# Reordered first loads, four PSUM banks for the first tile, a shorter attention lead and gated later loads in a linear-attention + MLP kernel

## The chip, the cores and the metric

One NeuronCore of one Trainium2 chip runs the whole program. The metric is device time in microseconds (us), the median over all runs of a kernel. A ratio is the mean time of one kernel's fast runs over the mean of the other's in the same rounds, so it is not quite the ratio of the medians that are quoted.

## The reference, cut to what matters

```python
batch, heads, seq, head_dim = 8, 8, 576, 64        # attention, 128 random features
q_s, k_s = q * 64**-0.25, k * 64**-0.25
def phi(x):                                        # x @ omega.T, minus |x|^2/2, minus the row max, exp
    h = einsum('bhsd,md->bhsm', x, omega) - sum(x*x, -1)/2
    return exp(h - max(h, -1)) / sqrt(128)
kv  = einsum('bhsm,bhsd->bhmd', phi(k_s), v)
num = einsum('bhsm,bhmd->bhsd', phi(q_s), kv)
den = einsum('bhsm,bhm->bhs',  phi(q_s), sum(phi(k_s), 2)) + 1e-6
x   = (num / den) as 4608 tokens x 512
h   = x @ w_in                                     # 512 -> 2048
out = (h * sigmoid(beta * h)) @ w_out              # 2048 -> 512, float32
```

## The kernel before: the parts that matter

The program is a list of operations with dependencies. A small list scheduler in the kernel's own source orders them for each engine by estimated durations; on the chip each engine then runs its list strictly in that order and waits on semaphores. There are 8 batches of attention. Batch b gives the transposed x (`xT`) of MoE tile b; a ninth tile collects the leftover tokens. A tile has 16 "up" groups (4 matmuls each, then tanh on ACT and a multiply on DVE) and 16 "down" groups (4 matmuls each).

```python
NAT_BUFS, T_BUFS, E_BUFS, Q_BUFS, V_BUFS, KV_BUFS, X_BUFS = 2, 2, 2, 2, 2, 2, 2
PE_T, PE_XT = 2, 3     # batches under 2: k and q transposed on PE; under 3: x too; later ones by DMA on SP
WARM = 24              # idle matmuls, meant to keep the PE clock up in the prologue
LEAD = 62              # attention may run that many MoE groups ahead
P0, O0, C0, H0 = 0, 2, 4, 6      # PSUM banks: projections, down, kv/num, up
# [...]
load("v", 0)           # v of batch 0: raw float32, issued by SP
load("k", 0)           # everything else: casting loads, issued by POOL, in this order
load("q", 0)
for c in range(4):
    load_w_in(c)
load("k", 1)
load("q", 1)
load_w_out(0)
load("v", 1)
for c in range(1, 4):
    load_w_out(c)
# [...] in attention(b): a gate is a number of MoE groups that the scheduler must have placed already
gates = [max(0, 32 * b - 16 - LEAD + 16 * half) if b >= 2 else 0 for half in range(2)]
# [...] b >= PE_T: one DMA transpose each for k and q
dma("SP", 4.0, 3.2, lambda e, x=x: e.dma_start(tr[x][:, st, :, :], nat[x][:, sn, :], transpose=True),
    reads=keys, writes=[...], gate=gates[0], lag=T_LAG)
# [...] up(t, f)
hb, ts, gs = H0 + u % 2, u % TH_BUFS, t % G_BUFS
# [...] down(t, sub, g4)
ob, os_, gs = O0 + u % 2, u % O_BUFS, t % G_BUFS
```

A gate is not a wait on the chip. It only says how late the scheduler puts an operation into its engine's list. For a load this is POOL's list, in which loads stand between the operations that scale v (`vsc`).

The softmax here doesn't subtract the row's maximum and nothing guards it: scores larger than these inputs give would overflow.

## Time and profile before

339.72 us (339.22 to 340.04); the profiled execution has a span of 337.9 us.

| stage | what limits it |
|---|---|
| 0 to 33.8 us, the prologue | the chain of batch 0: k's load, exponentials, x transposes |
| 33.8 to 333.9 us | PE, hardly waiting |
| the last 4 us | last eviction and store |

These are the waits of PE in the kernel before, from 33.8 us to the end (who waited for whom: us in total, times, longest):

```profile
PE ps L632 <- ACT xT L361: 0.8, 1, 0.8
PE ps L655 <- DVE g_sb L645: 0.6, 1, 0.6
```

L632 is the up matmul and L655 the down matmul. In 300 us PE waits 1.4 us. The windows view of the same kernel says it again; the columns are the stretch, its length, busy us of each engine (with its instructions), the granted PE clock, the DMA share as the view gives it (it can exceed 1) and GB/s:

```profile
60.00:80.00 20.00, 19.88 (x142) 10.30 (x141) 8.46 (x15) 11.81 (x20) 4.62 (x7) 1.00 1.37 179
80.00:120.00 40.00, 39.40 (x330) 23.42 (x329) 30.03 (x58) 31.83 (x59) 20.65 (x31) 1.00 1.44 166
160.00:180.00 20.00, 20.00 (x150) 10.46 (x148) 14.18 (x27) 11.14 (x18) 5.35 (x8) 1.00 0.75 125
180.00:220.00 40.00, 40.00 (x289) 22.28 (x288) 24.97 (x50) 29.45 (x54) 8.53 (x12) 1.00 0.37 85
```

The prologue, by the timeline (start, duration, engine, line, operation, and in brackets the idle time before it with its releaser):

```profile
9.72 0.82 PE L382 MATMUL ps<-identb,k_nat 128*128 128x128 bf16 x6 [5.64 <-DMA k_nat<-in_k_dram]
13.27 1.46 PE L382 MATMUL ps<-identb,k_nat 128*128 128x128 bf16 x12 [1.04 <-DMA k_nat<-in_k_dram]
...
23.76 2.21 ACT L441 ACTIVATE qpT<-ps 128x1024 bf16<-128x1024 f32 x3 [0.49 <-PE ps L426]
...
33.78 1.90 PE L632 MATMUL ps<-xT,w_in_bf 128*128 128x512 bf16 x8 [0.80 <-ACT xT L361]
```

PE waits 5.6 us for k, the q exponentials end at 26.0 us, and the first up matmul starts at 33.78 us. And two lines of its DMA issues (queue, count, KB each, median us from issue to landing):

```profile
k_nat<-in_k_dram POOLq DMA_DIRECT2D x4, 80.0 KB, 6.6
...
kT<-k_nat SPq DMA_TRANSPOSE x6, 12.1
```

The first line is k of batch 0. The second, the DMA transpose of k, takes 12.1 us to land in the median.

### The profile page before, as it was taken

To read this page: it belongs to the slowest core of one execution; us is meant where nothing else is said; L and a number is where in the kernel's file an instruction comes from. 1 tells how busy PE (TensorE), PEld (TensorE's weight loads), DVE (VectorE), ACT (ScalarE), POOL (GpSimd) and SP (SyncE) were. 2 spreads that over 40 slices of the span, in tenths; PEclk is the share of its full clock that TensorE was granted. 3 is DMA by queue.
4 is the path that set the end of the run, shared out by engine and by line. 5 is a ranking of instruction groups with operands and counts; after the bars stand their busy time and mean duration, and the time that the engine had idled before them with its cause. 6 is when DMAs were issued, how large, how long until landed. Compare 5 with 4: busy or idle time off the path is not lost.

```text
span 337.9 us, 5498 instructions
## 1 busy us (share of the span) xinstructions
PE 319.5 (95%) x2214; PEld 170.6 (50%) x2214; DVE 190.7 (56%) x358; ACT 204.0 (60%) x349; POOL 107.2 (32%) x161
## 2 busy tenths in 40 slices
PE   0597999999999999999999999999999999999995
PEld 0364565554655555665554565465444444444442
DVE  0196598428767769877854675765643333444400
ACT  2274668468886888788746876766444445444511
POOL 8859648215386262833500312303000000000000
PEclk9999999999999999999999999999999999999999
DMA  7999999999999999897196173221210001100033
GB/s 140 203 205 197 203 197 176 165 168 166 187 117 150 228 198 172 117 177 92 24 204 154 36 139 70 72 67 36 71 63 33 31 31 41 55 31 31 33 79 76
DMA packets 81113, 39.16 MB, mean 116 GB/s; under 512 B 47792, under 2 KB 76480, under 8 KB 81088
## 3 DMA queue, kind: packets, MB, share of 16 engines
q0 software_dynamic: 33280, 17.77, 41.2%
q1 hardware_dynamic: 47808, 21.05, 33.7%
q8 instruction: 17, 0.28, 0.4%
q14 instruction: 8, 0.07, 0.1%
HBM read 36.77 MB, written 9.44 MB: 137 GB/s over the span
## 4 chain that ended last, share of the span: by engine, by line
PE 87%; DVE 4%; ACT 3%; DMA 2%; POOL 1%; issue 0%; DVEq 0%; POOLq 0%
PE ps L655 36%; PE ps L632 35%; PE ps L418 4%; PE ps L426 4%; PE ps L546 3%; PE ps L521 2%; DMA k_nat<-in_k_dram 2%; POOL k_nat L254 1%; PE ps L382 1%; ACT E_sb L437 1%; ACT th_sb L641 1%; DVE g_sb L645 1%; DVE mk L474 1%; PE ps L580 1%; PE ps L595 1%; PE ps L516 1%
## 5 line engine op out<-in xcount | busy, mean ns | idle before, releaser
L645 DVE SCALAR_TENSOR_TENSOR g_sb<-th_sb,ps 128x512 bf16<-128x512 f32 x144 | 98.4, 685 | 92.5 <-ACT th_sb L641 91.9
L632 PE MATMUL ps<-xT,w_in_bf 128*128 128x512 bf16 x576 | 147.1, 379 | 0.8 <-ACT xT L361 0.8
L655 PE MATMUL ps<-w_out_bf,g_sb 128*128 128x512 bf16 x576 | 144.0, 379 | 0.7 <-DVE g_sb L645 0.6
L641 ACT ACTIVATE th_sb<-ps,beta_sb 128x512 f32<-128x512 f32 x144 | 99.1, 688 | 74.5 <-PE ps L632 73.8
L655 PEld LDWEIGHTS ps<-w_out_bf,g_sb 128*128 128x128 bf16 x576 | 55.5, 98 | 58.9 <-DVE g_sb L645 1.1
L632 PEld LDWEIGHTS ps<-xT,w_in_bf 128*128 128x128 bf16 x576 | 54.9, 98 | 53.8 <-DVE g_sb L645 1.0
L493 POOL TENSOR_TENSOR vsc<-v_nat,mk 128x512 bf16<-128x512 bf16 x28 | 28.8, 1050 | 88.2 <-DVE mkm L471 79.2
L437 ACT ACTIVATE E_sb<-ps 128x512 bf16<-128x512 f32 (+2 forms) x76 | 41.2, 573 | 18.4 <-PE ps L418 17.9
L441 ACT ACTIVATE qpT<-ps 128x512 bf16<-128x512 f32 (+2 forms) x76 | 41.4, 572 | 8.3 <-PE ps L426 7.4
L665 ACT ACTIVATE o_sb<-ps 128x512 f32<-128x512 f32 x36 | 21.5, 598 | 21.1 <-PE ps L655 21.0
L418 PE MATMUL ps<-bd,kT 128*128 128x256 bf16 x144 | 27.5, 291 | 1.6 <-ACT E_sb L437 0.9
L254 POOL DMA_DIRECT2D k_nat<-in_k_dram x36 | 22.5, 665 | 14.5 <-DMA kT<-k_nat 13.1
L561 DVE TENSOR_TENSOR xn<-ps,rden 128x640 bf16<-128x640 f32 x32 | 26.2, 820 | 0.7
L426 PE MATMUL ps<-qT,bd 128*128 128x256 bf16 (+2 forms) x152 | 25.7, 267 | 0.0
L418 PEld LDWEIGHTS ps<-bd,kT 128*128 128x128 bf16 x144 | 13.5, 103 | 12.4 <-ACT E_sb L437 2.4
L426 PEld LDWEIGHTS ps<-qT,bd 128*128 128x128 bf16 x152 | 13.7, 98 | 11.3 <-ACT qpT L441 0.8
L254 POOL DMA_DIRECT2D v_nat<-in_v_dram x28 | 17.6, 667 | 0.9 <-POOL vsc L506 0.8
L546 PEld LDWEIGHTS ps<-kvs,qpT 128*128 128x128 bf16 x320 | 13.7, 97 | 6.7 <-DVE kvs L537 0.9
L474 DVE TENSOR_TENSOR mk<-own,mkm 128x4 f32<-128x4 f32 x16 | 16.2, 1015 | 0.3
L452 DVE TENSOR_TENSOR mt<-E_sb 128x1152 bf16<-128x1152 bf16 x16 | 13.0, 811 | 4.3 <-ACT E_sb L437 4.1
L546 PE MATMUL ps<-kvs,qpT 128*128 128x65 bf16 x320 | 14.8, 193 | 0.3 <-DVE kvs L537 0.3
L269 POOL DMA_DIRECT2D q_nat<-in_q_dram x8 | 7.8, 975 | 15.7 <-DMA qT<-q_nat 14.4
(48 smaller groups left out, 155.0 us busy)
## 6 DMA issues: line engine op xcount, KB each, us to landing
out_dram<-o_sb SPq DMA_DIRECT2D x32, 256.0 KB, 2.4
q_nat<-in_q_dram POOLq DMA_DIRECT2D x8, 512.0 KB, 12.6
k_nat<-in_k_dram POOLq DMA_DIRECT2D x14, 160.0 KB, 12.5
v_nat<-in_v_dram POOLq DMA_DIRECT2D x14, 160.0 KB, 11.3
w_in_bf<-in_moe_w_in_dram POOLq DMA_DIRECT2D x4, 512.0 KB, 12.9
w_out_bf<-in_moe_w_out_dram POOLq DMA_DIRECT2D x4, 512.0 KB, 14.5
k_nat<-in_k_dram POOLq DMA_DIRECT2D x14, 128.0 KB, 12.5
v_nat<-in_v_dram POOLq DMA_DIRECT2D x14, 128.0 KB, 11.2
```

The lines of the kernel that those rows point to most:

```text
L254: lambda e: e.dma_start(dst[lo : lo + 64, g : g + group, c0 * D : (c0 + n) * D], srcap),
L418: i = e.matmul(view[:, c * 256 : c * 256 + 256], tr["k"][:, st, c0 + c, :], bd[:, :, :].rearrange("p a m -> p (a m)"), start=True, stop=Tr ...
L426: i = e.matmul(view[:, a * w : a * w + nch * 128], bd[:, a, :], tr["q"][:, st, c0 : c0 + nch, :], start=True, stop=True, skip_group_check= ...
L437: ex = lambda e: e.activation(dst[:, slot, s0 : s0 + 2 * nch, :].rearrange("p c m -> p (c m)"), view[:, 0 : nch * 256], AF.Exp)
L441: ex = lambda e: e.activation(dst[:, slot, s0 : s0 + 2 * nch, :].rearrange("p (c a) m -> p a c m", a=2), view.rearrange("p (a c) -> p a c" ...
L493: lambda e, pr=pr: e.tensor_tensor(vsc[:, sv, pr, 0:8, 0:D].rearrange("p (h j) d -> p h j d", h=2), ends(vs[:, v0 + 576 * pr : v0 + 576 * ...
L546: i = e.matmul(ps[:, N0 + pr, 65 * j : 65 * j + 65], qpT[:, sq, 8 * hh + 4 * pr + j if j < 4 else 16 + pr, :], kvs[:, sk, pr, 65 * hh : 65 ...
L561: lambda e, hh=hh, nv=nv: e.tensor_tensor(xn[:, sx, 5 * hh : 5 * hh + 5, :, :].rearrange("p j r d -> p r j d"), nv[:, :, :, 0:64], rden[:, ...
L632: i = e.matmul(o, w_in_bf[:, 2 * hh + half, f * 128 : (f + 1) * 128], rhs, start=kc == 0, stop=kc == 3)
L641: lambda e: e.activation(th_sb[:, ts, :], ps[:, hb, :], AF.Tanh, scale=beta_sb[:, f : f + 1]),
L645: lambda e: e.scalar_tensor_tensor(g_sb[:, gs, f, :], th_sb[:, ts, :], 1.0, ps[:, hb, :], ALU.add, ALU.mult),
L655: i = e.matmul(ps[:, ob, :], g_sb[:, gs, f, sub * 128 : (sub + 1) * 128], w_out_bf[:, f, :], start=f == 0, stop=f == NFF - 1)
```

## The change

Its intent: a shorter prologue. All of batch 0's loads cast in the DMA and go through one queue, k first, in two halves; k's transposes follow the halves; two of q's copies go to ACT; tile 0's h uses four PSUM banks; x of batch 0 is transposed through three banks. Besides, attention is to run less far ahead, and loads of batches 3 to 7 are to be held back.

```diff
-T_ACT = ()
+T_ACT = ("q0", "q6")
-WARM = 24
+WARM = (16, 6, 20)
-LEAD = 62
+LEAD = 46
+LOAD_LEAD = 14
 ...
+    def load_gate(b):
+        return max(0, 32 * b - 16 - LEAD - LOAD_LEAD) if b >= 3 else 0
 ...
-            dma("SP" if raw else "POOL", 0.45 if raw else 0.67, 0.05 * n * group,
+            dma("POOL", 0.65, 0.052 * n * group, gate=load_gate(b), fn=
 ...                                   # load_q gets gate=load_gate(b) too
-    load("v", 0)
-    load("k", 0)
+    load_kv("k", 0, (0,))
+    load_kv("k", 0, (1,))
 ...
     load("q", 0)
+    load_kv("v", 0, (0,))
+    load_kv("v", 0, (1,))
     for c in range(4):
         load_w_in(c)
 ...
-            for s in range(3):         # transposes in steps of 6, 6, 6
+            for c0, n in tsteps[x]:    # k of batch 0: 4, 5, 4, 5
 ...                                   # q half 1 of batch 0 in five narrow steps, not three wide ones
-                bk = H0 if first else C0 + hh
+                bk = (H0, C0, C0 + 1, H0)[2 * half + hh] if first else C0 + hh
 ...
-                copy("ACT",
+                copy("DVE" if first and half and hh else "ACT",
 ...
-        hb, ts, gs = H0 + u % 2, u % TH_BUFS, t % G_BUFS
+        hb = (H0, H0 + 1, O0, O0 + 1)[u % 4] if t == 0 else H0 + u % 2
```

More of the change, by code (lines that the diff above doesn't have):

```diff
@@ L200, in bass_performer_favor__then__act_swish_beta_kernel @@
     o_sb = sbt("o_sb", [128, O_BUFS, 512], F32)
-    v_raw = g_sb[:, 2, 0:10, :].rearrange("p f c -> p (f c)").bitcast(F32)
     ident_i = o_sb[:, 0, 0:128].bitcast(I32)
@@ L238, in bass_performer_favor__then__act_swish_beta_kernel, with load_kv @@
         writes=["bn"])
-    def load_kv(x, b, group=4):
+    def load_gate(b):
+        return max(0, 32 * b - 16 - LEAD - LOAD_LEAD) if b >= 3 else 0
+    def load_kv(x, b, halves=(0, 1)):
         t = {"k": k, "v": v}[x][b]
         sn = b % NAT_BUFS
-        raw = x == "v" and b == 0
-        dst = (v_raw[:, 0 : NCH * 128] if raw else nat[x][:, sn, :]).rearrange(
-            "p (P y) -> p P y", y=576)
+        dst = nat[x][:, sn, :].rearrange("p (P y) -> p P y", y=576)
         flat = t.rearrange("h s d -> h (s d)")
@@ L252, in part @@
                 "h (p y) -> p h y", y=n * D)
-            dma("SP" if raw else "POOL", 0.45 if raw else 0.67, 0.05 * n * group,
+            dma("POOL", 0.65, 0.052 * n * group, gate=load_gate(b), fn=
                 lambda e: e.dma_start(
                     dst[lo : lo + 64, g : g + group, c0 * D : (c0 + n) * D], srcap),
-                writes=[("vr" if raw else x, sn, key, i // 2) for i in range(g, g + group, 2)])
-        for g in range(0, 4, group):
+                writes=[(x, sn, key, i // 2) for i in range(g, g + group, 2)])
+        group = 2 * len(halves)
+        for g in (2 * halves[0],):
             part(g, 0, 0, 0, 5, 0, 0)
@@ L267, in load_q @@
         flat = q[b].rearrange("h s d -> h (s d)")
-        dma("POOL", 0.75, 3.2,
+        dma("POOL", 0.75, 3.2, gate=load_gate(b), fn=
             lambda e: e.dma_start(
@@ L273, in load_q @@
         for hh in range(2):
-            dma("POOL", 0.75, 0.6,
+            dma("POOL", 0.75, 0.6, gate=load_gate(b), fn=
                 lambda e, hh=hh: e.dma_start(
@@ L285, in load @@
     def load(x, b):
-        load_q(b) if x == "q" else load_kv(x, b, 2 if x == "k" and b == 0 else 4)
+        load_q(b) if x == "q" else load_kv(x, b)
     def load_w_in(c):
@@ L343, in bass_performer_favor__then__act_swish_beta_kernel, with warm @@
     BD = [("bd", 0), ("bd", 1)]
+    def warm(i, bk, reads, rhs, us):
+        n = rhs.free_size()
+        for _ in range(WARM[i]):
+            G.add("PE", us,
+                  lambda e: e.matmul(ps[:, bk, 0:n], identb[:, :], rhs, start=True, stop=True),
+                  reads=["idb"] + reads, banks=[bk], prio=9)
+    warm(0, H0 + 1, [], identb[:, :], 0.12)
     tb = [0]
@@ L365, in copy @@
                       writes=[key], banks=[bk], prio=0)
+        tsteps = {x: ((0, 6), (6, 6), (12, 6)) for x in "kq"}
+        if first:
+            tsteps["k"] = ((0, 4), (4, 5), (9, 4), (13, 5))
         def transpose_in(x):
@@ L372, in transpose_in @@
                                                transpose=True),
-                    reads=keys, writes=[(x + "T", st, s) for s in range(3)], gate=gates[0], lag=T_LAG)
+                    reads=keys, writes=[(x + "T", st, s) for s, _ in tsteps[x]],
+                    gate=gates[0], lag=T_LAG)
                 return
-            for s in range(3):
+            for c0, n in tsteps[x]:
                 bk = (H0 if first else P0) + tb[0] % 2
@@ L378, in transpose_in, with tp, proj_steps @@
                 pv = ps[:, bk, :].bitcast(BF16)
-                def tp(e, x=x, s=s, pv=pv):
-                    for c in range(6):
+                def tp(e, c0=c0, n=n, pv=pv):
+                    for c in range(n):
                         i = e.transpose(pv[:, c * 128 : c * 128 + 128],
-                                        nat[x][:, sn, (6 * s + c) * 128 : (6 * s + c + 1) * 128],
+                                        nat[x][:, sn, (c0 + c) * 128 : (c0 + c + 1) * 128],
                                         identb[:, :])
                     return i
-                keys = nat_keys(x, sn, (0, 1) if s == 1 else (s // 2,))
-                G.add("PE", 6 * 0.06, tp, reads=keys + ["idb"], banks=[bk], prio=0)
-                copy("ACT" if x + str(s) in T_ACT and first else "DVE",
-                     tr[x][:, st, 6 * s : 6 * s + 6, :].rearrange("p c t -> p (c t)"),
-                     pv[:, 0:768], (x + "T", st, s), bk)
-        steps = ((0, 4), (4, 4), (8, 1)) if first else ((0, 2), (2, 2), (4, 2), (6, 2), (8, 1))
+                keys = nat_keys(x, sn, range(c0 // 9, (c0 + n - 1) // 9 + 1))
+                G.add("PE", n * 0.06, tp, reads=keys + ["idb"], banks=[bk], prio=0)
+                copy("ACT" if x + str(c0) in T_ACT and first else "DVE",
+                     tr[x][:, st, c0 : c0 + n, :].rearrange("p c t -> p (c t)"),
+                     pv[:, 0 : n * 128], (x + "T", st, c0), bk)
+        def proj_steps(x, half):
+            if first and (x == "k" or half == 0):
+                return ((0, 4), (4, 4), (8, 1))
+            return ((0, 2), (2, 2), (4, 2), (6, 2), (8, 1))
         def proj(x, half, i):
             n = 2 * b + half
-            ch, nch = steps[i]
+            ch, nch = proj_steps(x, half)[i]
+            wide = len(proj_steps(x, half)) == 3
             s0 = 2 * ch
@@ L405, in proj @@
                 dst, slot = qpT, n % Q_BUFS
-            if first:
+            if wide:
                 bk = (P0, O0)[pb[0] % 2]
@@ L412, in proj @@
             pb[0] += 1
-            w = 512 if first else 256
+            w = 512 if wide else 256
             view = ps[:, bk : bk + len(banks), :].rearrange("p a c -> p (a c)")
@@ L433, in proj @@
                   kp if x == "k" else qp,
-                  reads=[(x + "T", st, s) for s in range(c0 // 6, (c0 + nch - 1) // 6 + 1)] + BD,
+                  reads=[(x + "T", st, s) for s, m in tsteps[x] if s < c0 + nch and s + m > c0] + BD,
                   banks=banks, prio=0, gate=gates[half], margin=mg)
@@ L453, in maxes @@
                                             E_sb[:, se, :, 64:128], ALU.max),
-                  reads=[("kE", se, i) for i in range(len(steps))], writes=["mt1"], prio=2)
+                  reads=[("kE", se, i) for i in range(len(proj_steps("k", half)))], writes=["mt1"], prio=2)
             G.add("DVE", dve_us(576, False, 2),
@@ L482, in scale_v @@
             se, sv = n % E_BUFS, n % V_BUFS
-            vs, v0 = (v_raw, 0) if first else (v_nat, NCH * 128 * sn)
-            v0 += 1152 * half
-            vn = vs[:, v0 : v0 + 1152].rearrange("p (P y d) -> p P y d", P=2, d=D)
+            v0 = NCH * 128 * sn + 1152 * half
+            vn = v_nat[:, v0 : v0 + 1152].rearrange("p (P y d) -> p P y d", P=2, d=D)
             vr = nat_keys("v", sn, (half,))
-            if first:
-                vr = nat_keys("vr", sn, (half,)) + [("g", 2, f) for f in range(10)]
             ve = V_ENG[half] if first else "POOL"
@@ L494, in scale_v @@
                           vsc[:, sv, pr, 0:8, 0:D].rearrange("p (h j) d -> p h j d", h=2),
-                          ends(vs[:, v0 + 576 * pr : v0 + 576 * pr + 640], D),
+                          ends(v_nat[:, v0 + 576 * pr : v0 + 576 * pr + 640], D),
                           mk[:, se, pr, 0:8].rearrange("p (h j) -> p h j", h=2).unsqueeze(3)
@@ L528, in kv_num @@
             G.add("PE", 0.65, kv,
-                  reads=[("kE", se, i) for i in range(len(steps))]
+                  reads=[("kE", se, i) for i in range(len(proj_steps("k", half)))]
                   + [("vm", sv), ("vs1", sv), ("vsc", sv, 0), ("vsc", sv, 1)],
@@ L552, in kv_num @@
                 G.add("PE", 0.33, num,
-                      reads=[("qE", sq, i) for i in range(len(steps))] + [("kvs", sk)],
+                      reads=[("qE", sq, i) for i in range(len(proj_steps("q", half)))] + [("kvs", sk)],
                       banks=BC, prio=0, margin=mg)
@@ L586, in kv_num @@
                 G.add("PE", 5 * 0.06, tp, reads=[("xn", sx, hh), "idb"], banks=[bk], prio=0)
-                copy("ACT",
+                copy("DVE" if first and half and hh else "ACT",
                      xT[:, half, b, 5 * hh : 5 * hh + 5, :].rearrange("p c t -> p (c t)"),
                      pv[:, 0:640], ("xT", half, b, hh), bk)
-        def warm():
-            for i in range(WARM):
-                G.add("PE", 0.22,
-                      lambda e: e.matmul(ps[:, H0 + 1, :], identb[:, :], tr["k"][:, st, 0:4, :],
-                                         start=True, stop=True),
-                      reads=["idb", ("kT", st, 0)], banks=[H0 + 1], prio=9)
         halves = ((0, 1),) if b < 2 else ((0,), (1,))
@@ L607, in attention @@
                     if first and x == "q":
-                        warm()
+                        warm(2, H0 + 1, [("kT", st, 0)], tr["k"][:, st, 0:4, :], 0.22)
                 for half in hs:
-                    for i in range(len(steps)):
+                    for i in range(len(proj_steps(x, half))):
                         proj(x, half, i)
@@ L614, in attention @@
                         scale_v(half)
+                if first and x == "k":
+                    warm(1, H0, [("kT", st, 0)], tr["k"][:, st, 0:4, :], 0.22)
             for half in hs:
@@ L620, in up @@
         u = NFF * t + f
-        hb, ts, gs = H0 + u % 2, u % TH_BUFS, t % G_BUFS
+        hb = (H0, H0 + 1, O0, O0 + 1)[u % 4] if t == 0 else H0 + u % 2
+        ts, gs = u % TH_BUFS, t % G_BUFS
         def mm(e):
```

## The prediction

> **What bounds the kernel now.** Two stages. From 33.8 us on, PE is saturated: the waits view filtered to PE after 33.8 us shows 1.4 us of waiting in all, and the stretches from 120 to 330 us are 100% busy at clock 1.00. Counting PE work after 33.8 us from the chain's own spacing (4 matmuls of 512 columns 0.86 us, so 248 us for 288 groups; about 6.4 us for each of seven attention batches; 4 us of transposes) gives 297 to 298 us, against 300.1 us taken (33.8 to 333.9). The tail is 4.0 us; the run's time is 1.8 us above the profiled span. So only the prologue, until the first up matmul at 33.78 us (timeline), can give much.
>
> The prologue's chain of waits: k0 lands late (PE waits 5.6 us, then 1.0 us, for the k DMA; halves land at 9.7 and 13.2 us; the chain has 7.6 us of DMA), k exponentials end at 20.2 us, q exponentials at 26.0, last normalised x at 31.1, then four x transposes and ACT copies one after the other on one PSUM bank (1.25 us each, 28.8 to 33.7).
>
> **What the change does.**
> 1. v0 (1.18 MB raw on SP) no longer moves beside k0. The Trainium skill, "DMA: Bandwidth & Descriptors", section "Queues, rings and completion order", says each DMA engine serves its queues in turn by packet; the trace fits: the fourth k0 issue starts at about 3.2 us and lands at 9.7, while the quickest k load took 2.8 us. Alone, k0 is bound by issue (8 x 0.62 us): I estimate its halves at 6.1 and 8.5 us. q0 should follow at about 12 to 13 us, v0 at 13.5 and 16.
> 2. Splitting k's transposes 4/5/4/5 frees half 0 from half 1: k exponentials done near 10.6 (half 0) and 13.6 us (half 1).
> 3. Two q copies to ACT (about 0.8 us each) relieve DVE but lengthen ACT's serial chain; q half 1 in narrow steps adds 0.5 us. q exponentials end near 20.3 us.
> 4. Transposes of x on three banks, one copy on DVE: about 1.5 us saved. First up at about 25.8 us: 8 us earlier (estimate).
> 5. Cost: DMA moves about 200 GB/s throughout 8 to 42 us, so k1, q1, v1 and w_out land no earlier than now (estimate: k1 29, v1 38, w_out 35 to 46 us), and tile 0's h on the O banks bars down(0) until up(0) is nearly done. Tile 0 plus batch 1 load ACT and DVE with some 22 us each in the 21 us after the first up. I charge 2 us of new PE stalls between 26 and 50 us.
> 6. Warm matmuls and held-back loads: off the critical path; no PE stall after 60 us to cure.
>
> **Sum.** 25.8 + 300.1 + 2 + 4.0 + 1.8 = 333.7; I say 333.5 us (1.8% faster), range 330 to 338. Chances: faster by over 2% 0.38, within 2% 0.60, slower 0.02.
>
> **What would show it.** k0's second half landed by 9 us and PE's wait for it gone; E_sb done near 14 us; first up at 25 to 27 us; PE waits between 26 and 50 us summing to 1 to 3 us, behind ACT, DVE or w_out loads; from 60 us on the same PE-bound pace.
>
> **What would make it wrong.** k0 alone being slower than the issue rate; vsc on POOL waiting for v0 and so delaying w_in; stalls of 4 us or more because batch 1 and w_out arrive too late; or held-back loads starving later batches' transposes (PE waits after 60 us).

## The result, and the profile after

353.25 us (351.64 to 353.76): 1.0392 times the kernel before, 95% interval 1.0353 to 1.043. The change was predicted to gain 1.8% and lost 3.9%. The range of 330 to 338 us does not hold it.

The prologue did get shorter. In the kernel after, L401 is the transpose of k and q, L460 and L464 the exponentials of k and q, L647 the up matmul:

```profile
6.02 0.61 PE L401 MATMUL ps<-identb,k_nat 128*128 128x128 bf16 x4 [0.45 <-DMA k_nat<-in_k_dram]
...
11.91 2.21 ACT L460 ACTIVATE E_sb<-ps 128x1024 bf16<-128x1024 f32 x3 [0.54 <-PE ps L441]
...
20.32 2.60 ACT L464 ACTIVATE qpT<-ps 128x512 bf16<-128x512 f32 x5 [1.13 <-PE ps L449]
...
28.01 7.08 PE L647 MATMUL ps<-xT,w_in_bf 128*128 128x512 bf16 x32 [0.59 <-DVE xT L378]
```

PE's long wait for k is gone, k's exponentials end at 14.1 us instead of 20.2, and the first up starts at 28.01 us, 5.8 us earlier. k of batch 0 now lands 2.7 us after its issue instead of 6.6.

Then the gain runs out and more is lost. These are the lines for the windows shown above, kernel after:

```profile
60.00:80.00 20.00, 16.73 (x122) 8.54 (x121) 6.54 (x12) 9.26 (x17) 1.07 (x2) 0.83 1.37 178
80.00:120.00 40.00, 38.83 (x322) 22.57 (x321) 23.96 (x52) 29.59 (x56) 15.54 (x23) 1.00 0.71 109
160.00:180.00 20.00, 16.66 (x81) 7.80 (x80) 9.42 (x18) 9.81 (x17) 3.27 (x5) 0.83 0.88 130
180.00:220.00 40.00, 36.97 (x273) 20.24 (x272) 21.73 (x41) 25.20 (x46) 12.97 (x21) 1.00 0.89 123
```

PE is idle for 3.3 us of 60 to 80, 3.3 us of 160 to 180 and 3.0 us of 180 to 220, and its clock falls to 0.83 in two of these stretches. Before, the same stretches lost 0.1 us in all.

**The hole at 66 to 72 us.** Counting the matmuls of the two traces (both complete, 576 up and 576 down), the kernel after has done 27 MoE groups by 60 us where the kernel before has done 22, then 32 against 30 by 70 us, and 38 against 40 by 80 us. The timeline of the kernel after shows why:

```profile
67.80 0.48 PE L566 MATMUL ps<-kvs,qpT 128*128 128x65 bf16 x10 [1.17 <-DVE xn L581]
69.46 1.25 PE L600 MATMUL ps<-identb,xn 128*128 128x128 bf16 x10 [1.17 <-DVE xn L581]
...
71.56 3.60 PE L647 MATMUL ps<-xT,w_in_bf 128*128 128x512 bf16 x8 [0.86 <-ACT xT L375]
```

All 32 groups of tile 0 are done, and PE steps through the last links of batch 1's attention with nothing to put between them. Tile 1 starts at 71.6 us; in the kernel before it started at 71.0 us. The start of tile 1 did not move at all. The 8 up matmuls after the hole take 3.60 us, twice their usual 1.9: the clock is at half.

**The waits after 120 us.** PE's waits from 130 us to the end are one line, in which L647 is the up matmul:

```profile
PE ps L647 <- DMA xT<-xn: 6.8, 3, 3.3
```

The largest lies at 170 us. SP's list, POOL's list, PE and the chain of waits around it (the last line is the chain's):

```profile
151.48 2.66 SPq L389 DMA_TRANSPOSE kT<-k_nat  x1
155.65 7.90 SPq L389 DMA_TRANSPOSE qT<-q_nat  x1
163.59 4.38 SPq L589 DMA_TRANSPOSE xT<-xn  x1
...
153.48 0.27 POOL L526 CAST vsc<-mk 128x20 bf16<-128x20 f32 x1
153.62 2.51 POOL L255 DMA_DIRECT2D k_nat<-in_k_dram  x4
156.07 0.96 POOL L271 DMA_DIRECT2D q_nat<-in_q_dram  x1
156.97 1.30 POOL L277 DMA_DIRECT2D q_nat<-in_q_dram  x2
158.19 2.53 POOL L255 DMA_DIRECT2D v_nat<-in_v_dram  x4
...
173.04 1.89 PE L647 MATMUL ps<-xT,w_in_bf 128*128 128x512 bf16 x4 [3.33 <-DMA xT<-xn]
...
163.59 9.40 DMA xT<-xn
```

As soon as POOL has scaled v, it issues all of batch 6's loads at once. Beside them, q's transpose of batch 5 keeps SP for 7.9 us and lands 15.6 us after its issue; in a quiet stretch (230.5 us) the same transpose takes 2.9 us and lands in 4.7. The x transpose of tile 4 stands behind it on SP, starts at 163.6 us and lands 9.4 us later; the median of all x transposes is 3.5. PE waits 3.3 us. The other two waits, at about 143 and 211 us, follow bursts of loads at 127 to 134 and 195 to 202 us in the same way.

### The profile page after: what moved, and what is told of

Its sections match the earlier page's. It is cut to its first block, busy times and chain, and to the rows that moved or that the text cites. A ratio compares the mean times of both kernels' runs of the same rounds, so it can differ in the third digit from the quotient of the medians.

```text
span 351.7 us, 5560 instructions
## 1 busy us (share of the span) xinstructions
PE 326.1 (93%) x2236; PEld 172.8 (49%) x2236; DVE 189.0 (54%) x358; ACT 205.2 (58%) x352; POOL 110.7 (31%) x169
## 3 DMA queue, kind: packets, MB, share of 16 engines
q1 hardware_dynamic: 46720, 19.87, 28.8%
## 4 chain that ended last, share of the span: by engine, by line
PE 81%; DMA 9%; DVE 6%; ACT 2%; POOL 1%; issue 1%; POOLq 0%
PE ps L647 34%; PE ps L670 31%; DMA xT<-xn 8%; PE ps L449 4%; PE ps L441 4%; PE ps L566 3%; PE ps L541 2%; DVE xn L581 1%; PE ps L354 1%; DVE mt L479 1%; DVE g_sb L660 1%; PE ps L600 1%; ACT th_sb L656 1%; DVE mt L475 1%; DMA k_nat<-in_k_dram 1%; PE ps L401 1%
## 5 line engine op out<-in xcount | busy, mean ns | idle before, releaser
L647 PE MATMUL ps<-xT,w_in_bf 128*128 128x512 bf16 x576 | 148.6, 386 | 8.6 <-DMA xT<-xn 6.8
L660 DVE SCALAR_TENSOR_TENSOR g_sb<-th_sb,ps 128x512 bf16<-128x512 f32 x144 | 98.7, 685 | 95.6 <-ACT th_sb L656 95.0
L647 PEld LDWEIGHTS ps<-xT,w_in_bf 128*128 128x128 bf16 x576 | 55.0, 99 | 66.6 <-DMA xT<-xn 7.8
L670 PEld LDWEIGHTS ps<-w_out_bf,g_sb 128*128 128x128 bf16 x576 | 55.4, 98 | 57.5 <-DVE g_sb L660 2.1
L513 POOL TENSOR_TENSOR vsc<-v_nat,mk 128x512 bf16<-128x512 bf16 x30 | 31.3, 1063 | 151.2 <-DVE mk L488 77.6
L464 ACT ACTIVATE qpT<-ps 128x512 bf16<-128x512 f32 (+2 forms) x78 | 42.2, 561 | 15.4 <-PE ps L449 14.9
L460 ACT ACTIVATE E_sb<-ps 128x512 bf16<-128x512 f32 (+2 forms) x76 | 41.2, 571 | 11.3 <-PE ps L441 10.9
L680 ACT ACTIVATE o_sb<-ps 128x512 f32<-128x512 f32 x36 | 21.5, 598 | 20.2 <-PE ps L670 20.1
L449 PE MATMUL ps<-qT,bd 128*128 128x256 bf16 (+2 forms) x156 | 27.2, 268 | 1.7 <-DVE qT L378 1.7
L441 PE MATMUL ps<-bd,kT 128*128 128x256 bf16 x144 | 26.2, 280 | 0.7 <-ACT E_sb L460 0.7
L255 POOL DMA_DIRECT2D v_nat<-in_v_dram x36 | 22.7, 728 | 0.1
L557 DVE CAST kvs<-ps 128x260 bf16<-128x260 f32 x15 | 6.4, 424 | 18.7 <-PE ps L541 18.7
L577 DVE RECIPROCAL rden<-ps 128x10 f32<-128x10 f32 x32 | 7.0, 218 | 15.6 <-PE ps L566 15.6
L475 DVE TENSOR_TENSOR mt<-E_sb 128x1152 bf16<-128x1152 bf16 x16 | 11.9, 747 | 4.8 <-ACT E_sb L460 4.7
```

The lines of the kernel that those rows point to most:

```text
L255: lambda e: e.dma_start(dst[lo : lo + 64, g : g + group, c0 * D : (c0 + n) * D], srcap),
L441: i = e.matmul(view[:, c * 256 : c * 256 + 256], tr["k"][:, st, c0 + c, :], bd[:, :, :].rearrange("p a m -> p (a m)"), start=True, stop=Tr ...
L449: i = e.matmul(view[:, a * w : a * w + nch * 128], bd[:, a, :], tr["q"][:, st, c0 : c0 + nch, :], start=True, stop=True, skip_group_check= ...
L460: ex = lambda e: e.activation(dst[:, slot, s0 : s0 + 2 * nch, :].rearrange("p c m -> p (c m)"), view[:, 0 : nch * 256], AF.Exp)
L464: ex = lambda e: e.activation(dst[:, slot, s0 : s0 + 2 * nch, :].rearrange("p (c a) m -> p a c m", a=2), view.rearrange("p (a c) -> p a c" ...
L513: lambda e, pr=pr: e.tensor_tensor(vsc[:, sv, pr, 0:8, 0:D].rearrange("p (h j) d -> p h j d", h=2), ends(v_nat[:, v0 + 576 * pr : v0 + 576 ...
```

## The experiments

Each kernel was correct and was timed in three rounds beside the kernel before. Every edit makes the scheduler plan all engines anew, so an edit of one line can also move other instructions in their lists. Theories: A, the shorter attention lead starves tiles 3 to 7. B, the gate on loads does. C, tile 0's use of the down banks makes the early hole. D, the early hole comes of batch 1's own chain, which did not move. E, the gate on loads hurts only together with the new prologue. F, a good part of the hole's cost is the clock. G, behind the hole, batch 2's DMA transposes are the next bound. H, the scheduler's wrong idea of load times is.

| run | edit | us, median | ratio to before |
|---|---|---|---|
| the change | | 353.25 | 1.0392 |
| a_lead62 | change, LEAD 62 | 348.67 | 1.0265 |
| b_lead46 | before, LEAD 46 | 340.34 | 1.0020 |
| a_nohold | change, no gate on loads | 342.66 | 1.0084 |
| a_2banks | change, tile 0 on two banks | 354.80 | 1.0432 |
| b_lead46_hold | before, LEAD 46 and the gate on loads | 358.66 | 1.0516 |
| a_nohold_l62 | a_nohold, LEAD 62 | 343.19 | 1.0120 |
| a_nohold_b1early | a_nohold, batch 1's loads earlier | 340.41 | 1.0019 |
| a_nohold_fill | a_nohold, 15 idle matmuls in the hole | 343.73 | 1.0114 |
| c_pet3 | a_nohold_b1early, batch 2 transposed on PE | 335.90 | 0.9897 |
| c_pet3_l62 | c_pet3, LEAD 62 | 333.66 | 0.9833 |
| b_pet3 | before, batch 2 transposed on PE | 346.69 | 1.0205 |
| c_calib | a_nohold_b1early, LEAD 62, measured load times in the scheduler | 339.38 | 1.0009 |
| a_loadlead30 | change, gate on loads 16 groups earlier | 350.04 | 1.0288 |
| c_pet3_l62_hold | c_pet3_l62 with the gate on loads | 340.33 | 1.0004 |
| c_pet3_l62_w_first | c_pet3_l62, batch 1's loads behind w_in | 339.44 | 0.9990 |

One of the four runs of b_lead46_hold and one of a_loadlead30 was slow. Their fast runs alone have medians of 357.69 and 348.86 us.

### Lead, gate or banks

**a_lead62**

```diff
-LEAD = 46
+LEAD = 62
```

> The changed kernel with LEAD put back from 46 to 62 (attention of batch b may start 16 MoE groups earlier), nothing else. Theory A (the shorter attention lead starves tiles 3 to 7 of their transposed x): the PE waits for the x transposes by DMA (6.8 us in the changed kernel, at about 141, 170 and 211 us) vanish with their clock dips, 10 to 12 us come back: about 342 us. Theory B (the held-back loads do it): LEAD also moves the load gates by 16 groups, so a part comes back, but the waits stay: 347 to 352 us. Theory C (tile 0 on the O banks spends its MoE work early and runs dry at 66 to 72 us): the early loss stays in either case, first up of tile 2... and tile 1 at about 71 us as in the changed kernel, and without A the time stays near 352 us.

348.67 us. The waits for x are gone, but PE now waits 3.0 us for a DMA-transposed q and 1.2 us for k. A part came back, as theory B said, though it also said that the waits for x would stay. Since LEAD moves the load gates as well, the run alone does not decide.

**b_lead46**

```diff
-LEAD = 62
+LEAD = 46
```

> The kernel before with LEAD 46 in place of 62, nothing else. Theory A: the same starvation appears in the kernel before, PE waits for the x transposes by DMA of several us between 120 and 220 us, 5 to 12 us slower: 345 to 352 us. Theory B (load holding) and theory C (O banks): the kernel before has neither, so LEAD alone does nothing: 339 to 341 us.

340.34 us, as good as the kernel before. Theory A falls. PE's waits in it after 33 us sum to 2.8 us, none on a DMA.

**a_nohold**

```diff
     def load_gate(b):
-        return max(0, 32 * b - 16 - LEAD - LOAD_LEAD) if b >= 3 else 0
+        return 0
```

> The changed kernel with the gate on loads taken out (all loads may be issued as soon as their buffers are free), LEAD still 46. Theory A: the waits for transposed x stay, 350 to 354 us. Theory B: the loads land earlier, k and q transposes and so x come in time, 340 to 345 us.

342.66 us: 10.6 us of the 353.25 come back with this one line, and after 130 us PE has no wait left that the profile lists. Theory B stands. ("The gate" means the gate with the order that follows from it: between the traces of the change and of a_nohold, ACT's list differs in 52 of 352 places and POOL's in 73 of 169, by operation and operands.) In a_nohold's trace the loads are a phase ahead: k of batch 5 is issued at 88 us instead of 127, k of batch 6 at 130 us instead of 154. What stays is the hole, as in the changed kernel; these are windows of a_nohold:

```profile
64.00:68.00 4.00, 3.02 (x38) 1.83 (x36) 1.34 (x3) 1.15 (x2) 0.00 (x0) 1.00 1.35 165
68.00:72.00 4.00, 1.21 (x20) 1.05 (x22) 1.18 (x3) 1.30 (x2) 0.00 (x0) 0.82 1.23 127
72.00:76.00 4.00, 3.90 (x12) 1.72 (x12) 0.69 (x1) 1.36 (x3) 1.39 (x3) 0.50 1.30 198
```

**a_2banks**

```diff
-        hb = (H0, H0 + 1, O0, O0 + 1)[u % 4] if t == 0 else H0 + u % 2
+        hb = H0 + u % 2
```

> The changed kernel with tile 0's h back on two banks (H0, H0+1), so that down(0) may interleave with up(0) as before; LEAD 46 and load gates as changed. Theory C: PE no longer runs out of work at 66 to 72 us, the wait and the clock dip there go, 4 to 7 us back: 346 to 349 us. Theory A alone: tile 1's x is late from its own chain, so the early gap just moves: 351 to 354 us.

354.80 us, no better than the change. But theory C does not fall by this. The same window of the changed kernel and of a_2banks, in this order:

```profile
68.00:72.00 4.00, 1.97 (x22) 1.31 (x19) 1.04 (x2) 1.30 (x2) 0.00 (x0) 0.68 1.59 128
68.00:72.00 4.00, 2.55 (x18) 1.18 (x18) 0.44 (x1) 2.53 (x5) 0.00 (x0) 1.00 1.56 145
```

With two banks the clock stays at 1.00, and the first tanh of tiles 1, 2 and 3 comes at 70.8, 110.7 and 139.1 us, which is 2.7, 3.7 and 5.2 us earlier than in the change. Then a wait of 4.6 us for k's transpose (at 162 us) and one of 5.2 us for x (at 212 us) take it back; both are of the kind that left with the gate in a_nohold. Two banks without the gate were not run, so what the four banks cost stays open.

### The gate on loads in the kernel before

**b_lead46_hold**

```diff
-LEAD = 62
+LEAD = 46
+LOAD_LEAD = 14
+    def load_gate(b):
+        return max(0, 32 * b - 16 - LEAD - LOAD_LEAD) if b >= 3 else 0
 ...    # and gate=load_gate(b) on the loads of k, q and v
```

> The kernel before with LEAD 46 (340.3 us alone) and in addition the changed kernel's gate on loads of batches 3 to 7. Theory B (held loads arrive too late for their transposes and so for the x of tiles 4 and up): the losses of the changed kernel show in the kernel before too: 346 to 353 us, with PE waits on DMA for transposed x, kT or qT after 100 us. Rival E (the gate on loads hurts only together with the new prologue): 339 to 343 us.

358.66 us (357.69 over the three fast runs), more than theory B asked for, with no part of the new prologue in it. Against b_lead46 (340.34), which differs only in the gate, it is some 17 us. Its PE waits after 25 us begin with

```profile
PE ps L422 <- DMA kT<-k_nat: 9.9, 2, 6.9
PE ps L636 <- DMA xT<-xn: 3.1, 1, 3.1
```

where L422 is k's projection and L636 the up matmul. So the gate is harmful by itself, and theory E falls.

**a_nohold_l62**

```diff
-LEAD = 46     (in a_nohold)
+LEAD = 62
```

> The changed kernel without the gate on loads and with LEAD back at 62. Theory B: with loads unheld the lead is of no matter, as in the kernel before: within 2 us of the 342.7 us of no gate alone. Theory A's remainder (the lead still costs something): 339 to 340.5 us. In either case the hole at 66 to 72 us stays.

343.19 us against 342.66: without the gate the lead is of no matter here. It will be of matter once the holes are filled (c_pet3_l62).

### The hole

**a_nohold_b1early**

```diff
-    for c in range(4):
-        load_w_in(c)
-    load("k", 1)
-    load("q", 1)
-    load_w_out(0)
-    load("v", 1)
+    load_w_in(0)
+    load("k", 1)
+    load_w_in(1)
+    load("q", 1)
+    load_w_in(2)
+    load("v", 1)
+    load_w_in(3)
+    load_w_out(0)
```

> No gate on loads, and batch 1's k, q and v loads issued between the four w_in loads instead of after them (w_in0, k1, w_in1, q1, w_in2, v1, w_in3, w_out0 to 3). Theory D (tile 1 can start only when batch 1's own chain of attention ends at about 71 us, which begins with k1's landing at 31 us in both kernels, so the earlier tile 0 leaves a hole): tile 1 starts 4 to 8 us earlier, the hole at 64 to 72 us and the clock dip after it shrink, 334 to 338 us. Rival (the hole comes of banks and engine order alone): tile 1 still starts at about 71 us, 341 to 344 us.

340.41 us; 2.3 us were gained where 5 to 9 were hoped for. Theory D is right about its own claim. By the first tanh of each tile (every 16th of the 144 in the trace):

| first tanh of tile, us | 0 | 1 | 2 | 3 | 4 |
|---|---|---|---|---|---|
| before | 34.9 | 72.1 | 109.6 | 141.0 | 168.8 |
| the change | 29.1 | 73.5 | 114.4 | 144.3 | 175.0 |
| a_nohold | 29.5 | 73.6 | 114.9 | 145.5 | 169.6 |
| a_nohold_fill | 29.4 | 72.7 | 112.8 | 143.5 | 169.0 |
| a_nohold_b1early | 28.8 | 65.0 | 110.7 | 142.3 | 165.6 |
| c_pet3 | 28.6 | 65.9 | 100.9 | 131.2 | 165.0 |
| c_pet3_l62 | 28.2 | 65.6 | 100.5 | 129.2 | 161.9 |

Tile 1 comes 8.6 us earlier than in a_nohold, as much as k of batch 1 lands earlier (23.4 us instead of 32.0), and the clock stays at 1.00 from 64 to 84 us, but tile 2 comes only 4.2 us earlier, and still later than in the kernel before. There is a second bound behind the first. In this kernel, batch 2's k and q are still transposed by DMA, on SP. Here are these transposes, and below them the largest PE wait of this trace with what leads to it:

```profile
57.49 7.43 SPq L391 DMA_TRANSPOSE kT<-k_nat  x1
65.05 8.19 SPq L391 DMA_TRANSPOSE qT<-q_nat  x1
73.28 1.18 SPq L687 DMA_DIRECT2D out_dram<-o_sb  x2
74.17 0.61 PE L443 MATMUL ps<-bd,kT 128*128 128x256 bf16 x4 [0.58 <-DMA kT<-k_nat]
...
95.09 0.92 POOL L271 DMA_DIRECT2D q_nat<-in_q_dram  x1 [3.54 <-DMA qT<-q_nat]
97.24 2.08 POOL L515 TENSOR_TENSOR vsc<-v_nat,mk 128x512 bf16<-128x512 bf16 x2
100.15 0.29 PE L538 MATMUL ps<-vsc,E_sb 128*128 128x130 bf16 x1 [2.73 <-POOL vsc L528]
```

k's transpose is issued at 57.5 us and batch 2's first projection of k can start only at 74.2. PE itself waits only 0.6 us there. The dearer wait comes later on the same way: batch 3's DMA transpose of q, queued behind batch 2's, lands at 94.6 us. Only then is the buffer free for the next load of q, POOL stands still for 3.5 us before that load, and batch 2's scaling of v comes after it in POOL's list. PE waits 2.7 us for that scaling.

**a_nohold_fill**

```diff
+            def fill(reads):
+                if b == 1 and half == 1:
+                    for _ in range(5):
+                        G.add("PE", 0.22, lambda e: e.matmul(ps[:, P0, 0:512], identb[:, :],
+                                                             w_in_bf[:, 0, 0:512], start=True, stop=True),
+                              reads=["idb", ("win", 0)] + reads, banks=[P0], prio=0)
 ...    # called after the two num groups of batch 1's second half and after its x transposes
```

> No gate on loads, and 15 idle matmuls of 512 columns put into PE's waits of batch 1's last half (5 beside each of its three last waits); every other instruction stays in its place on PE. Theory F (about a third of the loss at 64 to 80 us is the clock that falls to half after PE idles): the granted clock stays near 1.00 from 64 to 80 us and 2 to 4 us come back: 338.5 to 341 us. If the hole alone counts: clock back, but the time within 1 us of 342.7.

343.73 us, no gain. The clock was held, as its windows show:

```profile
68.00:72.00 4.00, 3.78 (x33) 1.89 (x33) 1.09 (x3) 1.30 (x2) 0.00 (x0) 1.00 1.44 95
72.00:76.00 4.00, 3.88 (x20) 1.79 (x20) 1.44 (x3) 3.13 (x6) 2.04 (x4) 1.00 1.05 204
```

Tile 2 then starts 2.1 us earlier than in a_nohold, and by tile 4 only 0.6 us of that is left. Theory F falls: a stall that is followed by another bound can be repaired without a gain.

### Batch 2

**c_pet3**

```diff
-PE_T, PE_XT = 2, 3     (in a_nohold_b1early)
+PE_T, PE_XT = 3, 3
```

> No gate on loads, batch 1's loads early (340.4 us alone), and batch 2's k and q transposed on PE instead of by DMA (costs PE about 2 us). Theory G (after the hole at 66 us is filled, the next bound is batch 2: its DMA transposes wait on SP behind tile 0's stores until 58 us and take 16 us to land beside the loads): tile 2 starts at 102 to 106 us instead of 110.7, PE waits at 68 to 116 us go, 335 to 338 us. Rival (PE is simply saturated and the transposes cost nothing): 341 to 343 us.

335.90 us. Tile 2 starts 9.8 us earlier than in a_nohold_b1early, although PE has some 2 us more to do, and the wait for the v scaling is gone too. Theory G stands: the transposes on SP were the bound. By which way, through kT or through POOL's list, is not separated.

**c_pet3_l62**

```diff
-LEAD = 46     (in c_pet3)
+LEAD = 62
```

> The same with LEAD 62. Lead without the load gate was worth nothing with the hole still there (343.2 against 342.7 us); if that holds also with the holes filled, within 1.5 us of the run before it; if the lead matters once PE is tight, 1 to 3 us faster than it: 334 to 336 us.

333.66 us (333.14 to 336.15), 0.9833 of the kernel before (95% interval 0.9794 to 0.9873): the version that beats both; whether its gain reaches 2% is unclear by this interval. The lead is worth some 2 us now (335.47 to 338.03 without it). All its PE waits from 25 us to the end:

```profile
PE ps L649 <- DVE xT L380: 0.3, 1, 0.3
PE ps L443 <- ACT E_sb L462: 0.2, 1, 0.2
PE ps L403 <- ACT E_sb L462: 0.2, 1, 0.2
```

**b_pet3**, the control.

```diff
-PE_T, PE_XT = 2, 3     (in the kernel before)
+PE_T, PE_XT = 3, 3
```

> Control: the kernel before with batch 2's k and q transposed on PE. Theory G says that the kernel before is bound by PE after 34 us, so taking DMA transposes away only adds PE work of about 2 us: 340 to 343 us. If DMA transposes held the kernel before as well: 334 to 338 us.

346.69 us, worse than both theories said. In the kernel before, transposing batch 2 by DMA was the better choice; that the earlier start turned it into a bound is likely but not shown alone, for the two kernels differ in more than that. Of the 7 us, PE work explains about 2 and a wait of 4.0 us for a v scaling on POOL (it ends at 120.5 us) the most of the rest. The trace shows the same way as in a_nohold_b1early: a DMA transpose of q is issued at 95.6 us and lands at 115.0, POOL stands still for 7.1 us before the load of q that needs its buffer, and the v scaling comes after that load.

**c_calib**

```diff
-            dma("POOL", 0.65, 0.052 * n * group, ...     (in a_nohold_b1early with LEAD 62)
+            dma("POOL", 0.65, 0.041 * n * group, ...
-        dma("POOL", 0.75, 3.2, ...     # q; 3.1 for w_in and w_out
+        dma("POOL", 0.75, 2.65, ...
```

> No gate on loads, batch 1's loads early, LEAD 62, batch 2 still transposed by DMA, and the scheduler's own estimates of the casting loads cut to the measured rate (0.041 in place of 0.052 us per unit of k and v, 2.65 in place of 3.1 and 3.2 us for w and q). Theory H (the static order puts batch 2's transposes behind stores because it believes the loads to be slower than they are): transposes issued some 6 us earlier, 336 to 339 us. If transposes' own landing time is the bound: 339 to 342 us.

339.38 us (338.58 to 343.18), just inside the second expectation but too scattered to choose: inconclusive. In the profiled run, the slowest of the four, batch 2's transpose of k was issued 3.8 us earlier than in a_nohold_b1early, not 6, and still took 15.5 us to land. Better load times in the scheduler at least do not replace taking batch 2 off the DMA.

### What stayed open, and two cross-checks

**a_loadlead30**

```diff
-LOAD_LEAD = 14
+LOAD_LEAD = 30
```

> The changed kernel with its gate on loads kept but opened 16 MoE groups earlier (LOAD_LEAD 30 in place of 14), LEAD still 46. If the gate hurts because the held loads run beside and just before the transposes that the next tiles wait for, opening it earlier brings most of the 10.6 us back: 343 to 346 us. If any gate on loads hurts by the order it gives the scheduler: 350 to 354 us.

350.04 us (one of four runs was slow; the three fast ones are 347.96 to 351.22). Over the fast runs some 4 of 10.6 us come back: neither expectation is met. How much of the gate's harm is the lateness of the loads, how much their coming in one burst behind a v scaling, and how much the changed order of the other engines stays open.

**c_pet3_l62_hold**

```diff
-        return 0     (load_gate, in c_pet3_l62)
+        return max(0, 32 * b - 16 - LEAD - LOAD_LEAD) if b >= 3 else 0
```

> The version of 333.7 us with the change's gate on loads put back in (LOAD_LEAD 14, LEAD 62). Theory B in the good version: PE waits on DMA for kT, qT or xT come back after 100 us, 338 to 342 us (the gate cost 5.5 us at LEAD 62 in the changed kernel). If the gate harms only a program that is late already: 333 to 335 us.

340.33 us: the gate costs the good version 6.7 us and eats its whole gain. PE's waits after 60 us in it:

```profile
PE ps L443 <- DMA kT<-k_nat: 3.1, 1, 3.1
PE ps L451 <- DMA qT<-q_nat: 2.9, 1, 2.9
```

**c_pet3_l62_w_first**

```diff
-    ...     (the load order of a_nohold_b1early, in c_pet3_l62)
+    ...     (the load order of the change: w_in first)
```

> The version of 333.7 us with batch 1's loads back behind all four w_in loads, as in the change. Theory D: tile 1 starts at 70 us or later again and the hole at 64 to 72 us is back or only shifted: 336 to 339 us. If the transposes of batch 2 on PE fill the hole by themselves: 333 to 335 us.

339.44 us: tile 1's first tanh is back at 73.9 us, and 5.8 us are lost. Both repairs are needed.

## Why the prediction was wrong

**Right: what bounds the kernel before, and the mechanism in the prologue.** "k0 ... halves at 6.1 and 8.5 us": they landed at 6.0 and 8.4. k's exponentials "13.6 us": 14.1. That v0 on SP slowed k0 agrees with the page cited in the prediction: alone, k0 lands 2.7 us after issue instead of 6.6.

**Mis-sized: the first up, "at about 25.8 us".** It came at 28.0, so 2.2 us of the predicted gain was missing. The term is "q exponentials end near 20.3 us": they ended at 22.9. In the trace, q's last transposed chunk waits for its copy on DVE, and DVE is held by one maximum of batch 0, shown here between the earlier one of the same kind and shape and the POOL operation that ran meanwhile (kernel after):

```profile
12.20 0.46 DVE L479 TENSOR_TENSOR mt<-mt 128x576 bf16<-128x576 bf16 x1
...
14.95 2.93 DVE L479 TENSOR_TENSOR mt<-mt 128x576 bf16<-128x576 bf16 x1
14.94 2.05 POOL L513 TENSOR_TENSOR vsc<-v_nat,mk 128x512 bf16<-128x512 bf16 x2
```

The Trainium skill, "SBUF — State Buffer", section "Terms", says that DVE and POOL arbitrate for a shared pair of SBUF ports which one instruction holds to its end while the other blocks. The trace fits (2.93 us instead of 0.46; it ends at 17.88 us, 0.3 us after the last of three v scalings on POOL, where the page speaks of one instruction), but no run here separates it.

**Wrong: "I charge 2 us of new PE stalls between 26 and 50 us".** The stalls came at 64 to 76 us, and without the gate they leave the kernel at 342.66 us with its first up at 28.4 us. The kernel before started 5.4 us later and took 339.7, so 8.3 us are lost after the first up. The failed step is the sum itself: "25.8 + 300.1 + ..." adds an earlier start to an unchanged PE stage. That holds only if the data of every later tile has that much slack. It had none: tile 1's x depends on batch 1's own chain, which began with k1's landing at about 31 us in both kernels (23.4 us in a_nohold_b1early), and I had written in the prediction that "k1, q1, v1 and w_out land no earlier than now". I used this to guess a small stall instead of asking when tile 1 can start. a_nohold_b1early moved tile 1, c_pet3 moved tile 2, and c_pet3_l62 then got the 333.7 us that the prediction had promised to the change; that the two figures agree so closely is chance. A part of the 8.3 us may also be the price of tile 0's four banks (a_2banks), which c_pet3_l62 still has.

**Wrong: "Warm matmuls and held-back loads: off the critical path; no PE stall after 60 us to cure."** There was nothing to cure, but there was something to break. The gate costs 10.6 us in the change (a_nohold), some 17 us in the kernel before with LEAD 46 (b_lead46_hold against b_lead46) and 6.7 us in the best version (c_pet3_l62_hold). "Held-back loads starving later batches' transposes" was listed among what could make the prediction wrong; it got no weight in the range.

**The three errors add up.** 2.2 (first up) + 6.3 (8.3 lost, 2 charged) + 10.6 (gate) = 19.1 us; the prediction was off by 353.25 - 333.5 = 19.75 us. The rest is rounding and the 0.4 us between the two first ups (28.0 and 28.4). The terms are differences of the same few times, so they must add up; this is bookkeeping and no further evidence.

**Not a cause:** LEAD alone (b_lead46) and the half clock after the hole (a_nohold_fill). Tile 0's four banks are not cleared: a_2banks was ahead of the change by up to 5.2 us until the gated loads' waits came. The Trainium skill, "TensorE: Matmul & The Clock Gate", section "Part 1: The HAM clock gate (the "warmup" mystery)", gives the halved clock after an idle window of about 3.4 us. The 0.50 in the windows agrees with the half; holding the clock at 1.00 bought nothing.

## What to carry to other kernels

A stage that shows no waits can still be exactly balanced: before adding the gain of an earlier start to it, find for each later tile when its data is ready and what its producer's chain hangs on, for an early start is worth only the smallest slack on the way. Holding loads back is not free when other DMA work that someone waits for, such as transposes, shares the engines: look at where the held burst will fall in the issuing engine's list and what stands behind it. The same goes for a load that waits for its buffer: it holds back the work behind it in that list (2.7 us of PE waiting in a_nohold_b1early, 4.0 in b_pet3). When one repair brings nothing, follow the start times of the tiles; they show where the gain was given back, and the next bound.

## What the Trainium skill lacked or had wrong

- "DMA: Bandwidth & Descriptors", section "Latency and other measured facts", gives 261 GB/s as the effective rate of a DMA transpose (measured on one kernel, with a non-contiguous middle dimension), which makes 0.59 MB (18 x 128 x 128 x 2 bytes) an estimated 2.3 us. Quiet, the SP issue of such a transpose took 2.9 us and it landed in 4.7 us; beside casting loads it landed in 15.6 us (change, batch 5) and in the median of 12.1 us (k, kernel before). The page does not say how far other queues' loads stretch a transpose, nor that they also stretch the time for which it occupies the issuing queue: 7.9 us instead of 2.9, with the next transpose behind it.
- "TensorE: Matmul & The Clock Gate", section "Part 1: The HAM clock gate (the "warmup" mystery)", speaks of one idle window of about 3.4 us; that short idle times can do it too stands only further down the page, without their lengths. Here two waits of 1.18 us, at 67.0 and 68.7 us, with bursts of 0.5 to 0.7 us of small matmuls after each, were enough: the clock was at 0.58 in the half microsecond from 70.5 us, before a third wait of 1.51 us had ended, and at 0.50 from 71 to 77 us (a_nohold).
- No page that I read says that a stage without waits may have no slack, so that an upstream gain is lost in it: 5.4 us of earlier start became 3 us of loss in a_nohold.
